# Layer 2 of a two-layer MoE by seven block products: result additions one tile later, first products inside layer 1's last gate, weight steps in another order

## The chip, the cores and the metric

The kernel runs on one core of a Trainium2 chip. The core has a matrix engine (TensorE, "PE" in the rows; its weight loads are "PEld"), VectorE (DVE), ScalarE (ACT), GpSimd (POOL) and SyncE (SP), which here issues nearly all DMAs. Each engine takes its instructions in the order in which the program lists them; they meet only at semaphores. Matmuls write to PSUM, the other data lies in SBUF. The metric is the time of one execution on the device in microseconds (us).

## The reference

```python
attn_out = _attn_ref(q, k, v)                    # 4 x 8 heads, 576 pooled queries, 1152 keys, D = 64
x = attn_out.transpose(0, 2, 1, 3).reshape(2304, 512)
# layer 1
h = x @ w_in                                     # 2304 x 512 by 512 x 2048
x = (h - np.tanh(h)) @ w_out                     # 2048 x 512
# layer 2
h = x @ w2_in
y = (h * (1.0 / (1.0 + np.exp(-1.702 * h)))) @ w2_out
```

Everything is float32, and the kernel keeps nearly that precision: it splits each operand into a rounded high part and the rest (the low part) and multiplies high by high, high by low and low by high.

## The kernel before

The program has three parts: attention, layer 1 and layer 2. The order on each engine is the order in which the Python code emits instructions; jobs are put into lists by hand (`at(step, place, job)` in layer 2, `early(w, place, job)` for jobs that stand inside layer 1's last ten gates) and emitted when that place is reached.

**Layer 1** walks 40 steps w (4 quarters of the 2048 hidden columns, 5 blocks of tokens, 2 halves). In each, TensorE makes `h` (24 matmuls, L1069) and then the output product `y` of two steps earlier (24 matmuls, L1152); `gate` follows on ScalarE and VectorE, `split_g` (L1081 on ScalarE, L1083 on GpSimd) splits the result. L1172 adds `y` into the accumulator `xb`. The `y` of the last two steps is made by `tail`, after layer 2's first `h` products.

**Layer 2** (`second_layer`) has 12 steps i: 4 quarters q of 512 hidden columns times 3 groups of 768 tokens. A group's tokens are two sides of 384 (G); tokens, model columns and hidden columns are each cut in two, and `h` of these blocks is made by seven products instead of eight. The operands are sums and differences of blocks: of x (X1, X2, X3, X4, beside the raw X11, X21, X22) and of the weights (S1 to S4, beside A11, A12, A22).

- `h_product(i, n)`, n = 0 to 6 (L934), is 12 matmuls of 384 columns for each product, into the PSUM tiles a, b, c, b, a, c, b. `h_after(n)` follows each: a copy on ScalarE (L943) and additions on VectorE (L945 to L956) that build up the blocks of `h` in `work`. `h_product` 3 needs tile `b` emptied by L945, 5 needs `c` emptied by L947, 6 needs L949 and L950.
- `gate2` is a sigmoid on ScalarE (L961) and a multiplication on VectorE (L962), four of each a step. `round_g` (L966, ScalarE) and `low_g` (L971, GpSimd) split the result.
- `y_product(i - 1, m)`, m = 0 to 5 (L985), is 12 matmuls of 512 columns for 128 tokens. Two products share a PSUM tile: 0 and 1, 2 and 3, 4 and 5. The addition to the accumulator follows each: L999 on ScalarE in the first quarter (a copy), L1001 on VectorE after that.
- The PSUM pool `ps` has four buffers of two banks each; a, b, c and the three `y` tiles of a step go through them in turn.
- x operands: `combine` (L701, VectorE) forms the sums, `round_x` (L706, L708, ScalarE) makes the high part, `low_x` (L714, L717, GpSimd or VectorE) the low part. `keep` stores the finished operand of each of the three groups in DRAM, `fetch` loads it again for the later quarters.
- Weights: `load_piece` loads 64-bit raw values into one of two buffers (L121), `convert_steps` turns them into float32 in four steps on VectorE (L138, L144, L151, L158) with one on ScalarE (L137), `split` (L165, L166, L765, L766) splits output weights, and `form` combines and splits the input weights of a quarter (L789 combination, L800 high part on ScalarE, L803 low part on GpSimd).

In every step, `go` emits `h_product` and `h_after` 0 to 6 with the jobs of places h0 to h6, the gate, the jobs of y0, and then the six `y` products, each with its addition, with the jobs of y1 to y5. All that the diff moves lies in these places.

Of the kernel before, what the change touches and what calls it, by code (L numbers as in the profile page):

```python
# [28 lines left out]
def tile_pooled_attention_two_moe(  # L29
# [11 lines left out]
    nc = tc.nc  # L41
# [594 lines left out]
    def second_layer(mem, HL, work):  # L636
# [16 lines left out]
        def wops(at):  # L653
# [5 lines left out]
            mem[:, 0:OPX], mem[:, OPX:2 * OPX], mem[:, 2 * OPX:3 * OPX], mem[:, free:free + OPX])]  # L659
        wgroups = [wops(3 * OPX), wops(HL[2])]  # L660
# [4 lines left out]
        u2, u3 = (work[:, 2 * OPX + n * 2 * G:2 * OPX + (n + 1) * 2 * G].rearrange(  # L665
            "p (f t) -> p f t", f=2) for n in range(2))
        sig = u2, u3
# [4 lines left out]
        parks = f32(part(9 * W + OPX, DM)), f32(mem[:, 3 * OPX + 14 * OPW:HL[3]])  # L672
# [11 lines left out]

        raw_x = {X11: (0, 0), X21: (1, 0), X22: (1, 1)}

        def scratch(n, o):
            t = rbd[:, 0:2 * G] if n == 0 else rest[:, 0:2 * G] if o == X1 else rest[:, 2 * G:4 * G]
            return t.rearrange("p (c t) -> p c t", c=2)

        def combine(n, o):
            dst = scratch(n, o)
            get = {(k, side): pieces(n, k, side) for k in range(2) for side in range(2)}
            for i in range(len(groups[n])):
                cols = get[0, 0][i][0]
                x = {at: got[i][1] for at, got in get.items()}
                d = dst[:, :, cols]
# [3 lines left out]
                nc.vector.tensor_tensor(d, one, two, op=op)  # L701
# [26 lines left out]
        def build(n, fast=()):  # L728
            def first(o):
                if o not in raw_x:  # L730
                    combine(n, o)
                round_x(n, o)

            def low(o):
                low_x(n, o, nc.vector if o in fast else nc.gpsimd)
                keep(n, o)

            return lambda o: lambda: first(o), lambda o: lambda: low(o)

        def prepared(kind, qn, f, home=None):  # L740
# [22 lines left out]
            def split():  # L763
                w, t = weight("o", n), home.unsqueeze(1)
# [5 lines left out]
        def form(qn, fp, boxes):  # L770
            w = wgroups[fp]

            def t(j):
                got = held[2 * fp + j] if qn > NQ else f32(boxes[j]["t"][:])
                return got.rearrange("p (k f) -> p k f", k=2)

            def place(o):
                n = {S1: 0, S3: 1, S2: 0, S4: 0}[o] if qn == NQ else o - S1
                t = slack if qn == NQ else rest
                return t[:, n * 256:(n + 1) * 256]  # L780

            def combine_w(*ops):
                for o in ops:
# [5 lines left out]
                    nc.vector.tensor_tensor(place(o), one, two, op=op)  # L789

            def source(a, b):
# [3 lines left out]
                if b > a:  # L795
                    at_ = rest[:, (a - S1) * 256:(b - S1 + 1) * 256]
# [16 lines left out]
            one = [run(combine_w, S1, S3), run(high, S1, S1), run(high, S3, S3)]  # L813
            two = [run(low, S1, S1), run(low, S3, S3), run(high, A11, A12), run(high, A22, A22)]
            three = [run(combine_w, S2), run(high, S2, S2), run(low, S2, S2)]
            four = [run(low, A11, A12), run(low, A22, A22)]
            five = [run(combine_w, S4), run(high, S4, S4), run(low, S4, S4)]
            return one, two, three, four, five
# [15 lines left out]
        for qn in range(NQ, 2 * NQ):  # L834
            ins = [prepared("i", qn, f, held[f] if qn > NQ else None) for f in range(4)]
            outs = [joined(piece("o", qn * 4 + f)) for f in range(2)]
            outs += [prepared("o", qn, f, parks[f - 2])[0] for f in (2, 3)]
            fs = [form(qn, fp, [ins[2 * fp + j][1] for j in range(2)]) for fp in range(2)]
            p = (qn - 1 - NQ) * NG
            if qn == NQ:  # L840
                early(0, "end", outs[0][0])
                early(1, "end", outs[1][0])
                early(2, "convert", outs[0][1], outs[0][2], outs[1][1])
                early(3, "split", outs[0][3])
                early(3, "convert", outs[1][2])
                early(4, "split", outs[1][3])
# [426 lines left out]
```

## Time and profile before

| | |
|---|---|
| median of 3 runs | 1355.37 us (1354.94 to 1356.22) |
| the profiled execution | 1354.87 us; its span, from the first instruction to the last, 1353.1 us |
| TensorE matmul / weight load | 1213.0 us (90%) / 999.5 us (74%) |
| VectorE / ScalarE / GpSimd | 996.0 us (74%) / 650.2 us (48%) / 620.4 us (46%) |
| mean granted TensorE clock | 0.952 |
| attention and layer 1 up to its last four gates | to 749.7 us |
| layer 2's first `h` product / step 3's / step 11's | starts at 801.8 / 960.7 / 1289.9 us |

The shares are means over three parts with different limits: TensorE is near full up to about 750 us and has gaps after that. A matmul counts as busy while it waits for its data to pass through the array, so a busy TensorE need not be at its full pace, and where the granted clock is 0.5 the same work takes twice as long.

### The profile page before, as it was taken

To read this page: it belongs to the slowest core of one execution; us is meant where nothing else is said; L and a number is where in the kernel's file an instruction comes from. 1 tells how busy PE (TensorE), PEld (TensorE's weight loads), DVE (VectorE), ACT (ScalarE), POOL (GpSimd) and SP (SyncE) were. 2 spreads that over 40 slices of the span, in tenths; PEclk is the share of its full clock that TensorE was granted. 3 is DMA by queue.
4 is the path that set the end of the run, shared out by engine and by line. 5 is a ranking of instruction groups with operands and counts; after the bars stand their busy time and mean duration, and the time that the engine had idled before them with its cause. 6 is when DMAs were issued, how large, how long until landed. Compare 5 with 4: busy or idle time off the path is not lost. (4 is left out here: it accounts for less than half of the span.)

```text
span 1353.1 us, 23589 instructions
## 1 busy us (share of the span) xinstructions
PE 1213.0 (90%) x9504; PEld 999.5 (74%) x9504; DVE 996.0 (74%) x1127; ACT 650.2 (48%) x962; POOL 620.4 (46%) x409
## 2 busy tenths in 40 slices
PE   9999999999999999999999956765898588868887
PEld 7777777777778888898898746655787477757775
DVE  6788888888879999999999877956545656643432
ACT  4556655566557776656665553443332222221210
POOL 6788887887861343333323243534233312341211
PEclk9999999999999999999999988777998789988989
DMA  4232232322201011111111024554544356423502
GB/s 141 80 129 80 92 124 79 116 89 93 76 27 56 31 48 47 47 44 35 47 47 47 32 83 181 195 203 193 196 179 158 143 219 225 162 85 136 190 36 78
DMA packets 45837, 144.44 MB, mean 107 GB/s; under 512 B 12960, under 2 KB 13728, under 8 KB 45728
## 3 DMA queue, kind: packets, MB, share of 16 engines
q1 hardware_dynamic: 45184, 142.54, 29.0%
q8 instruction: 75, 1.23, 0.4%
q10 hardware_dynamic: 544, 0.39, 0.1%
q14 instruction: 34, 0.28, 0.1%
HBM read 116.13 MB, written 21.31 MB: 102 GB/s over the span
## 5 line engine op out<-in xcount | busy, mean ns | idle before, releaser
L985 PE MATMUL y<-big,mem 128*128 128x512 f32 x540 | 178.7, 436 | 70.3 <-DVE xb L1001 37.5
L338 DVE TENSOR_REDUCE mt<-mx 128x2 fp32r<-128x1024 f32 (+2 forms) x176 | 195.8, 1136 | 58.9 <-PE mx L326 36.3
L985 PEld LDWEIGHTS y<-big,mem 128*128 128x128 f32 x540 | 112.6, 213 | 105.4 <-DVE xb L1001 40.8
L413 POOL TENSOR_TENSOR sum<-sum,pf 128x576 f32<-128x576 f32 x126 | 185.1, 1469 | 9.9
L1152 PE MATMUL y<-mem,big 128*128 128x512 f32 (+1 forms) x780 | 186.2, 370 | 3.0 <-POOL mem L1083 2.8
L402 ACT ACTIVATE pf<-sc 128x576 f32<-128x576 f32 x288 | 173.9, 653 | 22.3 <-PE sc L396 10.7
L971 POOL TENSOR_TENSOR mem<-work,mem 128x768 fp32r<-128x768 f32 x35 | 67.2, 1936 | 255.6 <-ACT mem L966 255.6
L1152 PEld LDWEIGHTS y<-mem,big 128*128 128x128 f32 x780 | 143.1, 189 | 24.1 <-POOL mem L1083 4.5
L428 PE MATMUL acc<-pf,v 128*32 128x288 f32 x2304 | 146.3, 407 | 0.0
L1001 DVE TENSOR_TENSOR xb<-xb,y 128x512 f32<-128x512 f32 x54 | 37.0, 685 | 115.5 <-PE y L985 115.5
L428 PEld LDWEIGHTS acc<-pf,v 128*32 128x32 f32 x2304 | 71.6, 110 | 65.7 <-ACT pf L402 4.5
L1083 POOL TENSOR_TENSOR mem<-work,mem 128x1024 fp32r<-128x1024 f32 (+1 forms) x39 | 87.0, 2230 | 66.8 <-ACT mem L1081 66.8
L166 POOL TENSOR_TENSOR big<-wt,big 128x512 fp32r<-128x512 f32 x30 | 40.5, 1350 | 151.3 <-ACT big L165 151.3
L1069 PE MATMUL h<-mem,big 128*128 128x512 f32 (+1 forms) x470 | 105.9, 377 | 0.0
L1069 PEld LDWEIGHTS h<-mem,big 128*128 128x128 f32 x470 | 86.9, 188 | 14.2
L396 PE MATMUL sc<-qh,kh 64*128 64x288 f32 x576 | 91.5, 314 | 0.0
L396 PE MATMUL sc<-row,sel 64*128 64x288 f32 x576 | 85.0, 291 | 0.3 <-ACT row L373 0.3
L396 PE MATMUL sc<-qh,kl 64*128 64x288 f32 x576 | 85.0, 291 | 0.0
L396 PE MATMUL sc<-ql,kh 64*128 64x288 f32 x576 | 84.8, 291 | 0.0
L1130 ACT ACTIVATE work<-work 128x1024 f32<-128x1024 f32 (+1 forms) x40 | 39.1, 978 | 94.4 <-DVE work L1128 94.4
L961 ACT ACTIVATE work<-work 128x768 f32<-128x768 f32 x48 | 39.2, 840 | 91.4 <-DVE work L956 86.9
L445 ACT ACTIVATE u<-acc 128x576 f32<-128x576 f32 x30 | 19.6, 653 | 125.6 <-PE acc L437 125.6
(172 smaller groups left out, 2753.9 us busy)
## 6 DMA issues: line engine op xcount, KB each, us to landing
mem<-x SPq DMA_DIRECT2D x36, 768.0 KB
big<-x SPq DMA_DIRECT2D x27, 768.0 KB
raw<-in_moe_w_in_dram SPq DMA_DIRECT2D x32, 512.0 KB
raw<-in_moe_w_out_dram SPq DMA_DIRECT2D x32, 512.0 KB
v<-in_v_dram SPq DMA_DIRECT2D x16, 576.0 KB
x<-mem SPq DMA_DIRECT2D x12, 768.0 KB
kr<-in_k_dram SPq DMA_DIRECT2D x15, 576.0 KB
qr<-in_q_dram SPq DMA_DIRECT2D x15, 576.0 KB
```

The lines of the kernel that those rows point to most:

```text
L166: nc.gpsimd.tensor_tensor(lo, t, f32(hi), op=ALU.subtract)
L338: nc.vector.tensor_reduce(out, src, AX.X, ALU.max, negate=True)
L396: nc.tensor.matmul(sc[:, s, 0:HB], w[r], m[r, xs], start=(n == 0), stop=(n == 3))
L402: nc.scalar.activation(pf, sc[:, :, 0:HB], AF.Exp, scale=SCALE)
L413: nc.gpsimd.tensor_add(out, parts[p, x], new)
L428: nc.tensor.matmul(acc[32 * n:32 * n + 32, 0], pairs[p]["v"][:, s, t, 32 * h:32 * h + 32], new[t][:, s, :], start=(t == 0), stop=(t == KT ...
L961: nc.scalar.activation(sig[fp], h, AF.Sigmoid, scale=1.702)
L971: eng.tensor_tensor(g[:, :, 1], halves[n][:, fp], f32(g[:, :, 0]), op=ALU.subtract)
L985: nc.tensor.matmul(y, gts[2 * side + fp][:, j, r, 128 * t:128 * t + 128], wo[:, p, :], start=(k == 0), stop=(k == len(terms) - 1))
L1069: nc.tensor.matmul(hb[:, j, 0:TBS[b]], wi[:, c, w, :], x[r][c], start=(k == 0), stop=(k == 3 * NKC - 1))
L1083: eng.tensor_tensor(gt[:, :, 1, :], g, f32(gt[:, :, 0, :]), op=ALU.subtract)
L1152: nc.tensor.matmul(ys[m][:, 0:w], wo[j][:, p, m * 128:(m + 1) * 128], g[:, j, r, :], start=(fp == 0 and not low and j == p == 0), stop=(fp ...
```

## The change

The diff has these parts.

1. **y's additions.** In `go`, `y_product` returns its addition, and the addition of product m is emitted after product m + 1, that of the last after all six.
2. **First products in the last gate.** `h_product` 0, 1 and 2 of step 0, with their `h_after`, are emitted inside gate 59 (place "convert" of w = 9) and at its end, and no longer in `go`. TensorE's order stays as it was. In step 0, `h_after` uses parts of `xb[0]` in place of u2 and u3.
3. **x operands.** `build` has three kinds of jobs now (`first` combines, `high`, `low`); the combinations of the second group's X3 and X1 go to GpSimd; the low parts of the second and third group are all GpSimd's (VectorE made X11, X3, X2 and X4); four `keep` DMAs come later (`kept_later`).
4. **Weights.** The first quarter's input weights are loaded and converted two to four gates earlier, their combinations go to GpSimd, and each half `fp` has a scratch of its own (`sums`). Output weight 1 of that quarter is converted in step 0 and no longer in layer 1. The conversions of the next quarters move by some places.
5. **Step 0 and 1.** The split of step 0's gate comes in step 1 (half of it on VectorE), and the jobs of h0 to h6 of step 0 are emitted after products 3 to 6.

```diff
@@ second_layer
-        u2, u3 = (work[:, 2 * OPX + n * 2 * G:2 * OPX + (n + 1) * 2 * G].rearrange(
+        us = tuple(work[:, 2 * OPX + n * 2 * G:2 * OPX + (n + 1) * 2 * G].rearrange(
             "p (f t) -> p f t", f=2) for n in range(2))
...
-        slack = work[:, 12 * TB:]
+        sums = work[:, 3 * OPX:]
...
+        kept_later = {(2, X1): (1, "y4"), (2, X21): (1, "y5"), (2, X4): (2, "h1"), (2, X22): (2, "h1")}
...
         def build(n, fast=()):
             def first(o):
-                if o not in raw_x:
-                    combine(n, o)
+                combine(n, o, nc.gpsimd if n == 1 and o in (X1, X3) else nc.vector)
+
+            def high(o):
                 round_x(n, o)
...
             def place(o):
-                n = {S1: 0, S3: 1, S2: 0, S4: 0}[o] if qn == NQ else o - S1
-                t = slack if qn == NQ else rest
-                return t[:, n * 256:(n + 1) * 256]
+                n = {S1: 6, S3: 7, S2: 6, S4: 6}[o] if qn == NQ else 4 * fp + o - S1
+                return sums[:, n * 256:(n + 1) * 256]
+
+            eng = nc.gpsimd if qn == NQ else nc.vector
...
-                    nc.vector.tensor_tensor(place(o), one, two, op=op)
+                    eng.tensor_tensor(place(o), one, two, op=op)
...
-                for f in range(4):
-                    early(2 + f, "end", ins[f][0][0])
-                early(4, "convert", ins[0][0][1], ins[0][0][2], ins[1][0][1])
-                early(5, "convert", ins[1][0][2])
-                early(6, "start", *fs[0][0])
...
-                early(9, "start", *fs[1][0], *fs[1][1])
-                early(9, "split", *fs[1][2])
-                early(9, "convert", *fs[1][3], *fs[1][4])
-                plan = ((outs[2], 0, "h1", "h2"), (outs[3], 0, "h5", "y1"))
+                for w, f in ((0, 0), (1, 1), (2, 2), (3, 3)):
+                    early(w, "end", ins[f][0][0])
+                early(2, "convert", ins[0][0][1], ins[0][0][2], ins[1][0][1])
+                early(3, "convert", ins[1][0][2])
+                for w, js in ((4, fs[0]), (8, fs[1])):
+                    early(w - 1, "end", *js[0])
+                    early(w, "start", *js[1])
+                    early(w, "convert", *js[2])
+                    early(w + 1, "convert", *js[3])
...
+                plan = ((outs[1], 0, "h2", "h3"),)
...
+        early(9, "convert", *first(X4), lambda: h_product(0, 0), lambda: h_after(0, 0),
+              *high(X4), *low(X4), lambda: h_product(0, 1), lambda: h_after(0, 1),
+              lambda: h_product(0, 2))
+        early(9, "end", lambda: h_after(0, 2), *high(X22), *low(X22))
         for n in range(1, NG):
-            first, low = build(n, (X11, X3, X2, X4))
...
+            first, high, low = build(n, ())
...
+        first_u = xb[0][:, 0:2, :], xb[0][:, 2:4, :]
+
+        def h_after(i, n):
+            u2, u3 = us if i > 0 else first_u
...
         def go(tail):
+            adds = []
             for i in range(NP + 1):
                 if i < NP:
                     for n in range(7):
-                        h_product(i, n)
-                        h_after(n)
+                        if i > 0 or n > 2:
+                            h_product(i, n)
+                            h_after(i, n)
+                        if n == 2 and i == 1:
+                            low_g(0, nc.vector)
                         if n == 0 and i > 0:
                             round_g(1)
                             low_g(1)
-                        do(i, f"h{n}")
+                            if i == 1:
+                                round_g(0)
+                        if i > 0:
+                            do(i, f"h{n}")
+                        elif n > 2:
+                            for m in ((0,), (1, 2), (3, 4), (5, 6))[n - 3]:
+                                do(i, f"h{m}")
...
                 for m in range(6):
                     if i > 0:
-                        y_product(i - 1, m)()
-                    if m == 2 and i < NP:
+                        adds.append(y_product(i - 1, m))
+                        if m > 0:
+                            adds.pop(0)()
+                    if m == 2 and 0 < i < NP:
                         round_g(0)
                         low_g(0)
                     if m > 0:
                         do(i, f"y{m}")
+                if adds:
+                    adds.pop(0)()
```

The lines of the changed kernel are numbered anew: `y_product`'s matmul is L1011 there, its addition L1027, `h_product` L957, `h_after` L971 to L982, `combine` L704, the low parts of x L717 and L720, of weights L814, layer 1's additions L1212.

First, TensorE's queue at the first `y` tile of step 4 (y_10848 before, y_10847 after), with the semaphores that its instructions wait for. Before, from inside product 0 to the second tile:

```order
L985 MATMUL y_10848<-big,mem 128x512 [waits Pool_49] x2
L985 MATMUL y_10848<-big,mem 128x512 x4
L985 MATMUL y_10848<-big,mem 128x512 [waits DVE_49]
L985 MATMUL y_10848<-big,mem 128x512 x11
L985 MATMUL y_10880<-big,mem 128x512 [waits PE_49]
L985 MATMUL y_10880<-big,mem 128x512 x11
L985 MATMUL y_10880<-big,mem 128x512 [waits DVE_49]
```

After, from the same place on:

```order
L1011 MATMUL y_10847<-big,mem 128x512 [waits Activation_49] x2
L1011 MATMUL y_10847<-big,mem 128x512 x2
L1011 MATMUL y_10847<-big,mem 128x512 [waits Pool_49] x2
L1011 MATMUL y_10847<-big,mem 128x512 x16
L1011 MATMUL y_10878<-big,mem 128x512 [waits DVE_49]
L1011 MATMUL y_10878<-big,mem 128x512 x13
```

The wait for VectorE at the thirteenth matmul of a tile, the start of the odd product, is gone; one stands at the first matmul of the next tile, whose buffer others read before.

Second, VectorE's queue in gate 59, layer 1's last, and at layer 2's first products (`xb_69` is layer 1's result of token block 3, `rbd` a scratch, `b` and `c` PSUM tiles of `h`). Before:

```order
L701 TENSOR_TENSOR rbd<-rbd,xb_66 128x768
L789 TENSOR_TENSOR work<-wt 128x256 x2
L1111 SCALAR_TENSOR_TENSOR work<-work,h 128x2x384
L789 TENSOR_TENSOR work<-work,wt 128x256
...
L1172 TENSOR_TENSOR xb_69<-xb_69,y 128x512 x3
L789 TENSOR_TENSOR work<-wt,work 128x256
...
L701 TENSOR_TENSOR rbd<-xb_66,rbd 128x768
L1083 TENSOR_TENSOR mem<-work,mem 128x2x384
L945 TENSOR_TENSOR work<-rbd,b 128x768
```

After:

```order
L1151 SCALAR_TENSOR_TENSOR work<-work,h 128x2x384
...
L1212 TENSOR_TENSOR xb_69<-xb_69,y 128x512 x3
L704 TENSOR_TENSOR xb_67<-xb_66,rbd 128x2x384
L971 TENSOR_TENSOR xb_66<-rbd,b 128x768
L1168 SCALAR_TENSOR_TENSOR work<-work 128x2x384
L1171 SCALAR_TENSOR_TENSOR work<-work 128x2x384
L1173 COPY_PREDICATED work<-work 128x2x384
L973 TENSOR_TENSOR xb_66<-xb_66,c 128x768
L1123 TENSOR_TENSOR mem<-work,mem 128x2x384
```

The weight combinations (L789) have left VectorE, and the first addition of `h` stands before the gate's last three instructions and before the split, not after them.

Third, GpSimd's queue at the turn from gate 59 to step 0. Before:

```order
L717 TENSOR_TENSOR mem<-rbd,mem 128x768
L714 TENSOR_TENSOR mem<-xb_67,mem 128x768
L717 TENSOR_TENSOR mem<-work,mem 128x768
L714 TENSOR_TENSOR mem<-xb_67,mem 128x2x128
L714 TENSOR_TENSOR mem<-xb_68,mem 128x2x256
L714 TENSOR_TENSOR mem<-xb_69,mem 128x2x128
L714 TENSOR_TENSOR mem<-xb_68,mem 128x2x256
```

After:

```order
L720 TENSOR_TENSOR mem<-xb_67,mem 128x768
L717 TENSOR_TENSOR mem<-xb_67,mem 128x768
L704 TENSOR_TENSOR work<-xb_69 128x2x128
L704 TENSOR_TENSOR work<-xb_68 128x2x256
L704 TENSOR_TENSOR work<-xb_69,xb_67 128x2x128
L704 TENSOR_TENSOR work<-xb_68 128x2x256
L717 TENSOR_TENSOR big<-xb_67,big 128x2x128
L717 TENSOR_TENSOR big<-xb_68,big 128x2x256
L720 TENSOR_TENSOR big<-work,big 128x768
L720 TENSOR_TENSOR mem<-work,mem 128x768
L166 TENSOR_TENSOR big<-wt,big 128x512
L720 TENSOR_TENSOR big<-work,big 128x768
```

Between the end of the first group's operands and the first split of layer 2's gate, GpSimd now also has two combinations of the second group, its low parts that were VectorE's, and an output weight's split.

## Rows read from the trace of the kernel before

**Rows 1.** Busy time by stretch: engines' busy us (instructions), granted clock, DMA share, GB/s.

```profile
core 0 of [0], span 1353.1 us
...
700.00:750.00 50.00, 50.00 (x245) 44.23 (x244) 46.66 (x55) 30.94 (x39) 15.42 (x9) 1.00 0.16 53
749.72:801.79 52.07, 44.22 (x194) 36.60 (x192) 41.12 (x44) 26.93 (x34) 20.80 (x13) 0.93 0.14 56
801.79:960.67 158.88, 102.14 (x446) 90.17 (x444) 108.09 (x125) 61.74 (x92) 64.40 (x39) 0.81 0.44 169
960.67:1349.40 388.73, 320.81 (x1477) 276.28 (x1475) 194.78 (x234) 92.31 (x128) 100.71 (x58) 0.92 0.42 156
```

**Rows 2.** Timeline of TensorE in layer 1: start, us, instruction, count.

```profile
700.27 4.32 PE L1069 MATMUL h<-big 128*128 128x384 f32 x24
704.43 4.32 PE L1152 MATMUL y<-mem,big 128*128 128x384 f32 x24
...
749.72 5.60 PE L1069 MATMUL h<-mem,w 128*128 128x512 f32 x24
755.16 0.62 PE L1152 MATMUL y<-mem,w 128*128 128x512 f32 x2
```

**Rows 3.** TensorE's waits, 960.67 to 1353.1 us: total us, times, longest.

```profile
PE y L985 <- DVE xb L1001: 62.4, 25, 13.3
PE y L985 <- ACT xb L999: 3.8, 3, 2.4
PE y L985 <- ACT wa L137: 1.7, 2, 0.9
```

**Rows 4.** TensorE's waits, 749.72 to 960.67 us.

```profile
PE y L985 <- ACT xb L999: 28.2, 6, 14.6
PE a L934 <- POOL mem L803: 8.2, 1, 8.2
PE b L934 <- DVE work L945: 7.1, 2, 4.6
...
PE y L1152 <- POOL mem L1083: 2.0, 2, 1.2
```

**Rows 5.** Chain that ended last, in step 9: start, us, what.

```profile
1226.62 0.96 DVE work L956
...
1229.48 0.85 ACT work L961
...
1230.35 1.83 DVE work L962 x2
```

**Rows 6.** Timeline of TensorE, step 9, two odd `y` products: idle before and releaser.

```profile
1232.83 0.80 PE L985 MATMUL y<-w,mem 128*128 128x512 f32 x1 [3.49 <-DVE xb L1001]
...
1242.03 0.47 PE L985 MATMUL y<-w,mem 128*128 128x512 f32 x1 [0.87 <-DVE xb L1001]
```

**Rows 7.** Busy time by stretch, around these two products; columns as above.

```profile
1232.80:1238.20 5.40, 5.37 (x13) 4.22 (x14) 0.00 (x0) 0.00 (x0) 0.00 (x0) 0.50 0.00 0
1242.00:1247.00 5.00, 4.97 (x22) 4.15 (x23) 0.69 (x1) 0.00 (x0) 2.47 (x2) 1.00 0.02 5
```

**Rows 8.** Timeline of GpSimd and VectorE in step 1.

```profile
859.00 6.53 POOL L971 TENSOR_TENSOR mem<-work,mem 128x768 fp32r<-128x768 f32 x3
...
863.90 2.17 DVE L144 SCALAR_TENSOR_TENSOR wt<-raw,wt 128x512 int32<-128x512 int32 x1
...
900.32 0.69 DVE L144 SCALAR_TENSOR_TENSOR wt<-raw,wt 128x512 int32<-128x512 int32 x1
```

**Rows 9.** VectorE by line, 801.79 to 960.67 us: busy us, mean ns, idle before.

```profile
L158 DVE SCALAR_TENSOR_TENSOR wt<-raw,wt 128x512 int32<-128x512 int32 x10 | 12.5, 1246 | 0.3
...
L144 DVE SCALAR_TENSOR_TENSOR wt<-raw,wt 128x512 int32<-128x512 int32 x10 | 9.9, 994 | 0.3
```

**Rows 10.** Timeline of VectorE, where step 5's weights are combined.

```profile
1063.41 0.93 DVE L789 TENSOR_TENSOR work<-w 128x256 f32<-128x256 f32 x1 [3.60 <-POOL mem L803]
```

**Rows 11.** GpSimd by line and shape, 960.67 to 1349.40 us; columns as in rows 9.

```profile
L803 POOL TENSOR_TENSOR mem<-work,mem 128x1024 fp32r<-128x1024 f32 x4 | 9.4, 2356 | 9.6 <-ACT mem L800 9.6
L803 POOL TENSOR_TENSOR mem<-w,mem 128x512 fp32r<-128x512 f32 x4 | 5.9, 1478 | 20.0 <-ACT mem L800 20.0
```

**Rows 12.** Timeline of VectorE, the last addition.

```profile
1349.45 0.69 DVE L1001 TENSOR_TENSOR xb<-xb,y 128x512 f32<-128x512 f32 x1 [3.11 <-PE y L985]
```

More of the change, by code (lines that the diff above doesn't have):

```diff
@@ L658, in second_layer @@
             part(3 * W, OPX), part(3 * W + OPX, OPX), part(9 * W, OPX),
-            mem[:, 0:OPX], mem[:, OPX:2 * OPX], mem[:, 2 * OPX:3 * OPX], mem[:, free:free + OPX])]
-        wgroups = [wops(3 * OPX), wops(HL[2])]
+            *(mem[:, 7 * OPW + n * OPX:7 * OPW + (n + 1) * OPX] for n in range(3)),
+            mem[:, free:free + OPX])]
+        wgroups = [wops(0), wops(HL[2])]
         gts = [t.rearrange("p (j r t) -> p j r t", j=2, r=2) for t in (
@@ L700, in combine @@
                     X2: (d, x[0, 0], ALU.add), X4: (x[1, 0], d, ALU.subtract)}[o]
-                nc.vector.tensor_tensor(d, one, two, op=op)
+                eng.tensor_tensor(dst[:, :, cols], one, two, op=op)
         def round_x(n, o):
@@ L735, in low, with each @@
                 low_x(n, o, nc.vector if o in fast else nc.gpsimd)
-                keep(n, o)
-            return lambda o: lambda: first(o), lambda o: lambda: low(o)
+                if (n, o) not in kept_later:
+                    keep(n, o)
+            def each(fn):
+                return lambda *some: [lambda o=o: fn(o) for o in some]
+            return each(first), each(high), each(low)
         def prepared(kind, qn, f, home=None):
@@ L812, in form @@
                         + [run(low, *x) for x in parts])
[L813 to L818, printed above, removed]
+            return (
+                [run(combine_w, S1, S3)],
+                [run(high, S1, S1), run(high, S3, S3), run(high, A11, A12), run(high, A22, A22),
+                 run(low, S1, S1), run(low, S3, S3), run(combine_w, S2)],
+                [run(high, S2, S2), run(low, A11, A12), run(low, S2, S2), run(combine_w, S4),
+                 run(low, A22, A22)],
+                [run(high, S4, S4), run(low, S4, S4)])
         jobs = {}
@@ L839, in second_layer @@
+            fs = [form(qn, fp, [ins[2 * fp + j][1] for j in range(2)], homes)
+                  for fp in range(2)]
             p = (qn - 1 - NQ) * NG
             if qn == NQ:
[L841 to L846, printed above, removed]
-                for f in range(4):
-                    early(2 + f, "end", ins[f][0][0])
@@ new lines, in second_layer @@
+        early(5, "end", *first(X1))
+        early(6, "convert", *high(X1, X11), *low(X1))
+        early(6, "end", *low(X11), *first(X3))
+        early(7, "convert", *high(X3, X21), *low(X3))
+        early(7, "end", *low(X21), *first(X2))
+        early(8, "convert", *high(X2), *low(X2))
+        early(9, "convert", *first(X4), lambda: h_product(0, 0), lambda: h_after(0, 0),
+              *high(X4), *low(X4), lambda: h_product(0, 1), lambda: h_after(0, 1),
+              lambda: h_product(0, 2))
@@ L917, in second_layer @@
+        for (n, o), place in kept_later.items():
+            at(*place, lambda n=n, o=o: keep(n, o))
         for i in range(NG, NP):
```

100 lines of the change are left out of this document (52 added, 48 removed).

## The prediction

> **What bounds the kernel now.** I first cut the span into stages with the table of busy time by stretch [rows 1]. From 700 to 750 us, in the middle of layer 1, TensorE is busy all the time at a granted clock of 1.00. From 749.72 us on it is not: 44.2 of 52.1 us, then 102.1 of 158.9 (the turn from layer 1 to layer 2: steps 0 to 2), then 320.8 of 388.7 (steps 3 to 11). No other engine is near full in the last two stretches: VectorE 108.1 and 194.8, GpSimd 64.4 and 100.7. So after 749.72 us the kernel is bound neither by TensorE nor by another engine, but by TensorE's waits.
>
> What TensorE's own work would need is read from gap-free stretches. 24 matmuls of 512 columns take 755.16 - 749.72 = 5.44 us, and 24 of 384 columns 704.43 - 700.27 = 4.16 us [rows 2]. Layer 2 runs both shapes. Seven products `h` of 12 matmuls are 7 x 2.08 = 14.56 us; six products `y` of 12 are 6 x 2.72 = 16.32 us; a step is 30.88 us. Against that pace:
> - 749.72 to 801.79 holds the last four gates' `h` (two pieces of 512 columns, two of 384) and four `y` of 512, 24 matmuls each: 6 x 5.44 + 2 x 4.16 = 40.96 us. It took 52.07: 11.1 too many.
> - 801.79 to 960.67 holds step 0's seven products, layer 1's last two `y` (8.32) and two whole steps: 84.64 us. It took 158.88: 74.2 too many.
> - 960.67 to 1349.40 holds eight whole steps, the last seven `h` products and twelve `y`: 8 x 30.88 + 14.56 + 32.64 = 294.2 us. It took 388.73: 94.5 too many.
>
> Together 179.8 us that are no work of TensorE's. The lists of waits say for whom [rows 3, 4]. From 960.67 on it is almost only L1001, the addition of a `y` tile: 25 waits, 62.4 us. Before that it is ScalarE's addition L999 (28.2 us in 6 waits), then weight operands (L803), h's additions (L945) and layer 1's own work.
>
> The timeline of one ordinary step shows how a short addition costs that much [rows 6]. The second `y` product of a pair (1232.83) sat 3.49 us until L1001, and later odd products 0.87 us. The chain of that moment [rows 5] reads backwards: `y` waited for L1001, which stood on VectorE behind the gate (L962), which waited for ScalarE's sigmoid L961, which waited for L956, the last addition of `h`. TensorE needed none of these; it waited because products 0 and 1 share a PSUM tile and the addition of 0 was queued before product 1. Then comes the second price: after the 3.49 us wait the granted clock is 0.50 for 5.4 us (1.2 instead of 2.4 GHz), 2.7 us lost; around a wait of 0.87 us it stays 1.00 [rows 7].
>
> **What the change does, and its cost.**
> *The additions one tile later.* In the order before, every odd product waits for VectorE; in the order after only the first product of a tile does, for the tile's former readers. An addition now waits until both halves are written and is wanted when its PSUM buffer comes round again: six tiles a step go through four buffers, so `b` of the next step needs the buffer of products 0 and 1. Between the end of product 1 and that `b` lie four products and `a`, 4 x 2.72 + 2.08 = 13 us. The gate and its wait, 3.5 us, hide in that. No instruction is added. For steps 3 to 11 I take away all 94.5 us, and add again one short wait of 0.87 us in each of seven steps (3 to 9, where weights are still split and formed): 6 us. The two ends are 0, and a full 3.49 + 2.7 in each of eight steps, 50 us; the nearest row is the short one, since no `h` product waits in the list from 960.67 on.
> The price moves to the end: the last pair's two additions now both follow the last matmul, one more of 0.69 us [rows 12].
>
> *The form step.* Where weights are combined, before, VectorE waited 3.60 us for GpSimd, as both halves used one scratch [rows 10]; now each has its own. GpSimd's six subtractions, 2 x 2.36 + 2 x 1.48 and two smaller ones, under 10.7 us [rows 11], start during `y` products that last 16.3 us, so they fit.
>
> *Transfers.* The same bytes move in less time: steps 3 to 11 had 156 GB/s at a share of 0.42; in 294 us it is 206 GB/s, 0.56. Steps 0 to 2 had 0.44 and would have 0.44 x 158.9 / 102 = 0.69 [rows 1]. Not full, so I cost it at nothing; a late transfer would show as TensorE waiting for DMA, and [rows 3] has none.
>
> *The turn.* PE's order is the same. What moves is who prepares what, and when: weight block 0 of fp 0 and 1 is formed on GpSimd one or more gates earlier, the first x operands too; the first three `h` products' additions stand inside the last gate, so L945's late place (7.1 us of waits) and the weight wait (8.2) have no cause left [rows 4]. One weight block's conversion leaves layer 1 for step 0. The price: GpSimd takes over eight subtractions and two combinations of x from VectorE.
> That is where I expect a rest. In the trace the conversion step L144 takes 0.69 us alone and 2.17 while three GpSimd instructions of 6.53 us run [rows 8]; over the turn L144 has a mean of 0.994 and L158, of the same size, 1.246, that is 0.30 and 0.56 more, with GpSimd busy 64.4 / 158.9 = 0.41 of the time [rows 1, 9]. Per instruction with two SBUF inputs that is 0.7 to 1.4 us at a GpSimd that is always busy; I take 0.9, near the lower end, as the gate's multiplications stayed at 0.92 (two in 1.83) where GpSimd rested [rows 5].
> The Trainium skill ("SBUF — State Buffer", SBUF: two separate sides) says that VectorE instructions with two SBUF inputs and GpSimd's take turns on one port pair, whole instructions at a time; these rows agree. It speaks against moving work to GpSimd, and by it alone each such instruction would wait for one of GpSimd's.
> Between product 6 of step 0 and the additions that free the buffer for step 1's `c`, VectorE has about ten instructions of that kind (four conversion, four gate, two combination) at 0.7 to 0.95 us, L956 (0.96) and four additions of at most 0.69: 8 + 1 + 2.8 = 11.8 us. TensorE covers 8.32 + 2 x 2.08 = 12.5. GpSimd has some eleven instructions of 768 columns from the last gate on, at 6.53 / 3 = 2.18 each 24 us of about 28, a share of 0.85. With 10 x 0.9 x 0.85 = 7.6 us more they are 6.9 late, and the clock drop adds 2.7: 9.6. Step 1 has a similar list with fewer deadlines; I take 7.4. Together 17 us; the ends are 0, and the doubled price of all conversions (below).
> In layer 1's end I keep the waits for GpSimd (2.0 [rows 4]) and 1 us: 3.
>
> *Sum*, against the profiled execution, 1354.87 us (its span 1353.1 and 1.8 around it; the median is 1355.37, 0.5 more): 1354.87 - 11.1 - 74.2 - 94.5 + 0.7 = 1175.8, plus 3 + 17 + 6 = 1202.
>
> **The rivals.**
> *A. Nothing is left over.* TensorE runs gap-free to the end: 1176 to 1183. For it: each wait listed loses its cause. Against it: VectorE's 11.8 us under a cover of 12.5.
> *B. The turn becomes bound by VectorE and GpSimd together.* Steps 0 to 2 hold 9 conversions of four instructions; if each takes the 2.17 us of [rows 8] instead of the 1.12 that L144 and L158 have in the mean, VectorE needs 36 x 1.05 = 38 us more than its 108.1, less about 10 for the ten instructions that GpSimd takes over (at L956's 0.96): 136 instead of 84.6 us. Time: 1176 + 51 + 9 = 1236. This is the skill's rule taken to its end; the trace bears it out for single instructions, not for whole stages, as GpSimd also idles on ScalarE.
> *C. The wait comes back in every step*, at a PSUM buffer or an operand: an addition that stands behind the gate and a late conversion, and `b` or `c` of the next step waits. At the old price, 8 x (3.49 + 2.7) = 50 on top: 1252. For it: VectorE still works in order. Against it: 13 us of cover.
> *D. Slower: the clock.* If a TensorE that never rests were granted 1.2 GHz, its 379 us of work in the last two stretches (84.6 + 294.2) would take up to 379 more. It decides at 40%: (1355 - 1202) / 379. Against it: 50 us of full work at 1.00 in layer 1 [rows 1].
>
> **How the numbers follow.** The forecast, 1202, has 0.62, with its own range 1183 to 1222; A 0.07, B 0.20, C 0.08, D 0.03. All but D are far faster than the 0.2% (2.7 us) that a measurement of this kernel can tell from no change; D I split into 0.02 slower and 0.01 same. The range that holds 8 in 10 reaches from 1180 (part of A) to 1245 (most of B).
>
> **What would show it.** Right: from step 3 on, starts of `a` 31 us apart, no wait for L1001's successor over 1 us, clock 1.00 through the steps; TensorE's busy share after 750 us over 0.9; the last addition pair after the last matmul. The rest should stand at `c` or `b` of step 1 and in front of `y` of step 0, with VectorE's conversion steps near 2 us beside a busy GpSimd. Wrong: waits for DMA in the `h` products (fetches too late), waits of 3 us or more at a tile's first product in steps 3 to 11 (C), or a turn over 125 us (B).

## The result, and the profile after

The changed kernel takes 1218.29 us (median of 4 runs, 1217.81 to 1218.86) against 1355.48 (4 runs, 1354.94 to 1356.22): a ratio of 0.8988, 95% interval 0.8972 to 0.9003. Forecast: 1202, range 1180 to 1245. The profiled execution took 1217.97, its span 1216.2.

Lines are those of the changed kernel from here on: y's product is L1011 and its additions L1025 (ScalarE) and L1027 (VectorE), h's products are L957 and their additions L971 to L982, the gate's multiplication L988, the low parts of the gated values L997 and of the x operands L717 and L720, weights are combined at L800 and their low parts made at L814, a conversion is L138, L144, L151 and L158, and layer 1's last additions are L1212 (L1157 is an operation of its gate on VectorE).

Busy time by stretch of the changed kernel, columns as in [rows 1]: layer 1's end, the turn in three pieces (each ends where the next `a` starts) and as a whole, and steps 3 to 11:

```profile
749.72:798.34 48.62, 44.10 (x198) 36.97 (x196) 47.24 (x43) 28.69 (x38) 33.23 (x21) 0.96 0.25 92
798.34:827.88 29.54, 26.05 (x134) 25.47 (x132) 26.51 (x25) 13.43 (x21) 24.46 (x16) 0.88 0.39 140
827.88:870.69 42.81, 33.86 (x157) 29.38 (x157) 42.41 (x39) 19.92 (x27) 27.33 (x15) 0.92 0.48 174
870.69:914.40 43.71, 33.39 (x157) 29.59 (x156) 39.09 (x41) 20.77 (x34) 22.18 (x12) 0.92 0.74 289
798.34:914.40 116.06, 93.30 (x445) 84.44 (x444) 108.00 (x103) 54.11 (x81) 73.96 (x43) 0.91 0.56 209
914.40:1211.80 297.40, 295.86 (x1477) 266.15 (x1475) 205.67 (x243) 95.78 (x136) 113.93 (x63) 1.00 0.55 207
```

Steps 3 to 11 went from 388.73 us at a clock of 0.92 to 297.40 at 1.00, 3.2 above TensorE's own 294.2; from step 4 on `a` starts every 30.94 or 30.95 us. The turn went from 158.88 to 116.06, 31.4 above its 84.64. In the turn's second piece VectorE, the third pair of numbers, is busy for 42.41 of 42.81 us: a full engine stands behind TensorE's waits.

TensorE's waits in steps 3 to 11 of the changed kernel, in total, times and longest, where 25 waits of 62.4 us for L1001 stood [rows 3]:

```profile
PE b L957 <- DVE work L971: 1.1, 1, 1.1
PE b L957 <- DVE work L976: 0.2, 1, 0.2
PE c L957 <- ACT xb L1025: 0.2, 1, 0.2
```

The turn's long waits, from TensorE's timeline of the changed kernel (idle time before and releaser in brackets):

```profile
803.74 4.18 PE L957 MATMUL b<-big,mem 128*128 128x384 f32 x12 [3.13 <-DVE work L1157]
...
840.19 3.92 PE L957 MATMUL c<-big,mem 128*128 128x384 f32 x12 [6.67 <-DVE xb L1212]
...
876.04 2.38 PE L957 MATMUL b<-big,mem 128*128 128x384 f32 x12 [3.08 <-ACT xb L1025]
...
888.05 3.89 PE L957 MATMUL b<-mem 128*128 128x384 f32 x12 [6.62 <-DVE work L971]
```

Twelve matmuls of 384 columns start 2.08 us before the next product at full clock, and their row then shows 2.24 to 2.27; after three of these waits the row shows 3.9 to 4.2. The wait at 876.04 is put down to ScalarE, but leads back to VectorE as well: ScalarE's copy L1025 stands in its queue behind a rounding that had waited for VectorE's combination L704.

```profile
872.89 0.84 ACT L711 ACTIVATE mem<-work 128x768 fp32r<-128x768 f32 x1 [1.95 <-DVE work L704]
...
875.40 0.59 ACT L1025 ACTIVATE xb<-y 128x512 f32<-128x512 f32 x1
```

Of the 31.4 us, 22.8 are idle time (116.06 - 93.30) and 8.7 are TensorE's busy time above 84.64, most of it at a lower clock.

What the last long wait stands for is seen on VectorE and GpSimd just before it, in the timeline of the changed kernel:

```profile
877.90 6.47 POOL L997 TENSOR_TENSOR mem<-work,mem 128x768 fp32r<-128x768 f32 x3
878.42 2.05 DVE L138 TENSOR_SCALAR wt<-raw 128x512 int32<-128x512 int32 x1
880.50 2.20 DVE L144 SCALAR_TENSOR_TENSOR wt<-raw,wt 128x512 int32<-128x512 int32 x1
882.81 2.10 DVE L151 SCALAR_TENSOR_TENSOR wt<-wa,wt 128x512 f32<-128x512 f32 x1
884.33 2.25 POOL L997 TENSOR_TENSOR big<-work,big 128x768 fp32r<-128x768 f32 x1
...
884.95 2.18 DVE L158 SCALAR_TENSOR_TENSOR wt<-raw,wt 128x512 int32<-128x512 int32 x1
887.05 0.94 DVE L971 TENSOR_TENSOR work<-rbd,b 128x768 f32<-128x768 f32 x1
887.92 0.41 DVE L138 TENSOR_SCALAR wt<-raw 128x512 int32<-128x512 int32 x1
...
888.37 0.69 DVE L144 SCALAR_TENSOR_TENSOR wt<-raw,wt 128x512 int32<-128x512 int32 x1
```

One half of a weight conversion took 8.5 us (2.05 + 2.20 + 2.10 + 2.18) beside four operations of GpSimd; the first two operations of the next one, with GpSimd at rest, took 0.41 and 0.69. L971, for which TensorE waited, came right behind. At the end, the last two additions follow the last matmul, as predicted (1.28 us for both, against 0.69 in [rows 12]):

```profile
1211.81 1.28 DVE L1027 TENSOR_TENSOR xb<-xb,y 128x512 f32<-128x512 f32 x2 [4.16 <-PE y L1011]
```

### The profile page after: what moved, and what is told of

It is laid out like the page before. It is cut to its first block, busy times and chain, and to the rows that moved or that the text cites. A ratio compares the mean times of both kernels' runs of the same rounds, so it can differ in the third digit from the quotient of the medians.

```text
span 1216.2 us, 23601 instructions
## 1 busy us (share of the span) xinstructions
PE 1177.7 (97%) x9504; PEld 982.8 (81%) x9504; DVE 1010.9 (83%) x1108; ACT 648.4 (53%) x962; POOL 663.5 (55%) x428
## 4 chain that ended last, share of the span: by engine, by line
PE 74%; DVE 17%; ACT 4%; issue 2%; POOL 1%; DMA 1%; DVEq 0%; SPq 0%; POOLq 0%; ACTq 0%
PE y L1011 13%; PE sc L396 13%; PE acc L428 11%; PE h L1109 10%; PE y L1192 9%; PE b L957 5%; PE a L957 3%; PE mx L326 3%; PE c L957 3%; PE acc L437 3%; DVE wt L144 2%; DVE wt L151 2%; DVE work L1168 2%; DVE wt L158 1%; DVE work L1151 1%
## 5 line engine op out<-in xcount | busy, mean ns | idle before, releaser
L1011 PE MATMUL y<-big,mem 128*128 128x512 f32 x540 | 153.7, 390 | 1.2 <-ACT big L774 1.0
L997 POOL TENSOR_TENSOR mem<-work,mem 128x768 fp32r<-128x768 f32 x33 | 65.4, 2000 | 131.9 <-ACT mem L992 131.9
L1011 PEld LDWEIGHTS y<-big,mem 128*128 128x128 f32 x540 | 101.1, 188 | 22.6 <-ACT big L774 1.5
L158 DVE SCALAR_TENSOR_TENSOR wt<-raw,wt 128x512 int32<-128x512 int32 x64 | 75.3, 1177 | 2.0
```

What stands on the lines that cost most here:

```text
L158: nc.vector.scalar_tensor_tensor(out=t, in0=raw[:, :, 0], scalar=29, in1=t, op0=ALU.logical_shift_right, op1=ALU.bitwise_or,)
L997: eng.tensor_tensor(g[:, :, 1], halves[n][:, fp], f32(g[:, :, 0]), op=ALU.subtract)
L1011: nc.tensor.matmul(y, gts[2 * side + fp][:, j, r, 128 * t:128 * t + 128], wo[:, p, :], start=(k == 0), stop=(k == len(terms) - 1))
```

## The experiments

Theory: the lag of y's additions gives back the steps; the rest of the gain is the turn's, and the turn stays bound by VectorE, which GpSimd slows. Rivals: the order alone decides where TensorE waits; or VectorE's load alone does. Times are medians of 4 runs (the last run: 5), ratios are to the kernel before in the same session.

**1. The lag alone**, on the kernel before:

```diff
-                        y_product(i - 1, m)()
+                        adds.append(y_product(i - 1, m))
+                        if m > 0:
+                            adds.pop(0)()
```

> The kernel before with one part of the change alone: y's additions one tile later in layer 2. Theory 1 (steps 3 to 11 give about 94 us back by the lag alone, and the waits of the y products inside the turn go too, some 15 us more, while the form's wait of 3.6 us and the rest of the turn stay): 1235 to 1265 us, about 1250, and no wait of a y product over 1 us in steps 4 to 10. Rival (the lag only works together with the new order of operands, so that other waits appear where the additions' waits were): over 1285 us. Rival (the turn and layer 1's end are bound up with the lag as well): under 1235 us.

Measured: 1255.98 us, ratio 0.9271 [0.9255, 0.9286]. The lag alone is 99.2 of the 137 us. Turn, and steps 3 to 11, of this kernel:

```profile
801.93:933.52 131.59, 97.16 (x445) 88.53 (x444) 106.40 (x119) 55.78 (x83) 58.66 (x36) 0.86 0.53 202
933.52:1249.00 315.48, 301.03 (x1477) 271.18 (x1475) 207.10 (x240) 97.02 (x138) 111.69 (x62) 0.98 0.51 192
```

The turn lost 27.3 us, not 15, and the steps 73.3, not the 94 expected. What stays in the steps are mainly three waits, in steps 3, 6 and 9 (L945 and L1001 are L971 and L1027 of the changed kernel):

```profile
947.54 4.21 PE L934 MATMUL b<-mem 128*128 128x384 f32 x12 [7.49 <-DVE work L945]
...
1043.88 3.91 PE L934 MATMUL c<-big,mem 128*128 128x384 f32 x12 [3.39 <-DVE xb L1001]
...
1141.97 3.50 PE L934 MATMUL c<-big,mem 128*128 128x384 f32 x12 [3.38 <-DVE xb L1001]
```

**2. The change without the lag** (the same lines, undone in the changed kernel).

> The changed kernel with y's additions issued right behind each product, as before. Theory 1: the odd products' wait of 3.49 us and the five of 0.87 us come back in every step from 1 on, with the clock at its lower level behind them: about 9 us a step in steps 3 to 11 and some in steps 1 and 2: 1300 to 1325 us. Rival (the new order alone would have removed most of the waits): under 1270 us. If the parts add up, this run's loss against the changed kernel equals the gain of the lag alone against the kernel before.

Measured: 1324.69 us, ratio 0.9778 [0.9764, 0.9793]: 106.4 slower than the changed kernel. TensorE's waits in steps 4 to 11 of it:

```profile
PE y L1011 <- DVE xb L1027: 52.2, 25, 8.1
```

Again 25, as in [rows 3]. The other parts alone give 30.5 us; 99.2 + 30.5 falls 7.5 short of the whole of 137.2, so the parts help each other a little. Where the other parts gain and lose is seen by setting the changed kernel beside run 1: step 0 is 18.1 us shorter (29.54 against 47.62), step 1 2.5, layer 1's end 3.6, steps 3, 6 and 9 together 18, but step 2 is 5.0 us longer (43.71 against 38.71). Step 2 takes 31.35 us in run 7, so most of its excess hangs on GpSimd's low parts.

**3. One place for both forms' weight sums**, as before:

```diff
-  ... else 4 * fp + o - S1
+  ... else o - S1
...
-                    at_ = sums[:, 4 * fp * 256:4 * (fp + 1) * 256]
+                    at_ = sums[:, 0:4 * 256]
```

> The changed kernel with one place for the weight sums of both column pairs of a form in layer 2's later quarters, as before, instead of one for each. The lag alone showed waits of 3.39 us before c, with 1.6 us of lower clock behind each, in two steps with forms. Theory (these waits come from the second form's sums waiting for the first one's reads, with y's additions behind them on VectorE): they come back, 5.3 us each in steps 6 and 9, and perhaps a third in the turn's last step: 1227 to 1236 us. Rival (the order of the conversions decides and the place of the sums does not): 1217 to 1220 us.

Measured: 1232.74 us, ratio 0.9094 [0.9076, 0.9112], 14.5 slower. The wait of run 1 is back, in steps 6 and 9; here is step 6, VectorE first, TensorE below:

```profile
1009.68 0.95 DVE L800 TENSOR_TENSOR work<-w 128x256 f32<-128x256 f32 x1 [3.66 <-POOL mem L814]
...
1020.41 1.87 DVE L1027 TENSOR_TENSOR xb<-xb,y 128x512 f32<-128x512 f32 x3
```

```profile
1021.14 4.21 PE L957 MATMUL c<-big,mem 128*128 128x384 f32 x12 [3.38 <-DVE xb L1027]
```

VectorE waits 3.66 us for GpSimd to read the first form's sums, with y's additions queued behind; the lag moves that lateness to the `c` of the next step. Each of these two steps takes 37.1 us instead of 30.95; step 3 takes 35.8 instead of 33.3.

**4. The wait before step 1's `c` taken away by order alone**: layer 1's last products and additions are issued right behind the last h product of step 0, ahead of a half conversion and the gate.

```diff
+                        if i == 0 and n == 6:
+                            tail()
...
-                if i == 0:
-                    tail()
```

> The changed kernel with the last additions of layer 1 (L1212) put on VectorE ahead of half a weight conversion, the gate and a combination of step 0 instead of behind them, about 9 us of its queue. TensorE's order is unchanged. Theory VectorE-bound (it is busy 42.4 of 42.8 us from 827.88 to 870.69, so a wait that is taken away here comes back behind the next VectorE result): the wait of 6.67 us before c of step 1 goes, but another of 4 to 6 us stands before the next product that needs L971 or L975, and the time falls by only 0 to 4 us: 1214.5 to 1218.5. Rival (order alone): the wait of 6.67 us and the 1.8 us of lower clock behind it go and nothing comes back: 1208.5 to 1211.

Measured: 1218.33 us, ratio 0.8992 [0.8978, 0.9005]: no change. In TensorE's timeline of it the wait has moved on by one product:

```profile
834.19 2.24 PE L957 MATMUL c<-big,mem 128*128 128x384 f32 x12
843.17 4.21 PE L957 MATMUL b<-mem 128*128 128x384 f32 x12 [6.74 <-DVE work L971]
```

6.67 us went and 6.74 came: moving these additions forward gains nothing by itself. The new wait is not all a full VectorE, though. Just before L971 VectorE itself stood idle, for ScalarE's copy L969, which is queued behind a rounding that waits for VectorE's L704:

```profile
842.16 0.95 DVE L971 TENSOR_TENSOR work<-rbd,b 128x768 f32<-128x768 f32 x1 [1.66 <-ACT rbd L969]
```

So part of the turn is a chain through both queues; whether another order of ScalarE's queue would help was not run.

**5. The first products outside the last gate**: L971 of step 0 stands behind the gate's operations.

```diff
-  ... lambda: h_product(0, 0), lambda: h_after(0, 0), ... lambda: h_product(0, 2))
...
-                        if i > 0 or n > 2:
-                            h_product(i, n)
-                            h_after(i, n)
+                        h_product(i, n)
+                        h_after(i, n)
```

> The changed kernel with the first three products of layer 2 and what follows them on ScalarE and VectorE issued behind the last gate of layer 1 instead of inside it. TensorE's order is the same; what moves is L971's place on VectorE, behind three operations of the gate (about 4 us). Theory VectorE-bound: the second b of step 0 waits about 3 us longer, VectorE itself does the same work, and the time rises by 0 to 4 us: 1218 to 1222 us. Rival (the early products carry the gain at layer 1's end): over 1225 us.

Measured: 1218.30 us, ratio 0.8989 [0.8976, 0.9003]. In its timeline of TensorE (L955 and L969 are L957 and L971 here) a wait appears in step 0, and step 2 begins all the same at 871.65, against 870.69:

```profile
816.55 4.00 PE L955 MATMUL b<-mem 128*128 128x384 f32 x12 [7.44 <-DVE xb L969]
...
871.65 2.27 PE L955 MATMUL a<-big,mem 128*128 128x384 f32 x12
```

In return the wait before step 1's `c` fell from 6.67 to 1.88 us. It cost nothing because VectorE had the same work to do. So this place of the additions gains nothing by itself.

**6. Three conversions later in VectorE's queue.**

```diff
-                    (ins[2][0], 1, "y3", "y4"), (ins[3][0], 2, "h1", "h2"),
-                    (outs[0], 2, "h4", "h5"), ...
+                    (ins[2][0], 2, "h1", "h2"), (ins[3][0], 2, "h3", "h4"),
+                    (outs[0], 2, "h5", "h6"), ...
```

> The changed kernel with three weight conversions of VectorE moved back in its queue: one from ahead of L971 of step 2 to behind it, and the two after it by two or three products each. TensorE's order is unchanged. Theory VectorE-bound with some slack here (39.1 of 43.7 us busy from 870.69 to 914.40): the wait of 6.62 us before the second b of step 2 falls under 2 us, but the moved conversions delay the weight forms at step 2's end, whose results step 3 needs, so that 1 to 5 us remain of the 8: 1213 to 1217 us. Rival (order alone): 1208.5 to 1211 us.

Measured: 1227.06 us, ratio 0.9057 [0.9043, 0.9070]: 8.8 slower, which no theory had forecast. The wait of 6.62 us is gone, as expected, but the weights of step 3 come late:

```profile
913.01 1.01 PE L957 MATMUL a<-big,mem 128*128 128x384 f32 x2 [5.30 <-ACT mem L811]
...
922.26 1.65 PE L957 MATMUL a<-big,mem 128*128 128x384 f32 x4 [3.25 <-POOL mem L814]
```

With two smaller waits they come to 10.9 us. The forms are a chain over three engines behind the last conversion. The expectation had named the late forms, but from VectorE's slack had put them at 3 to 7 us, without the two engines behind it.

**7. GpSimd's load taken away.** The low parts of the x operands of groups 1 and 2 are left out (their products read what lay there before).

```diff
-                low_x(n, o, nc.vector if o in fast else nc.gpsimd)
+                if n == 0:
+                    low_x(n, o, nc.vector if o in fast else nc.gpsimd)
```

> The changed kernel without the low parts of the layer-2 operands of token groups 1 and 2: some 14 operations of GpSimd of 1.8 to 2.9 us in steps 0 and 1 are left out (their products then read what lay there before). VectorE's instructions are the same. Theory contention (VectorE's operations between two SBUF tiles are slower beside GpSimd): VectorE's busy time from step 0 to the end of step 2 falls from 108 us to 88 to 98, with the means of the conversion and gate operations near 0.7 and 0.95 us, and the time falls to 1198 to 1212 us. Rival (VectorE's load and its order alone): VectorE's busy time stays at 105 to 109 us and the time at 1216 to 1219 us.

Measured: 1200.26 us, ratio 0.8859 [0.8846, 0.8872], 18.0 faster. The turn, and one conversion operation by line (busy us, mean ns), of this kernel:

```profile
799.90:895.25 95.35, 88.52 (x446) 80.18 (x445) 88.10 (x102) 53.66 (x79) 38.17 (x25) 0.98 0.67 253
```

```profile
L158 DVE SCALAR_TENSOR_TENSOR wt<-raw,wt 128x512 int32<-128x512 int32 x8 | 5.5, 693 | 0.3
```

The same row of the changed kernel's turn:

```profile
L158 DVE SCALAR_TENSOR_TENSOR wt<-raw,wt 128x512 int32<-128x512 int32 x8 | 13.6, 1694 | 0.3
```

VectorE, with the same instructions, is busy 19.9 us less, and the turn is 20.7 us shorter. Not every operation gains: L138's mean rose from 0.93 to 1.19 us beside what GpSimd still does. GpSimd's busy time falls by 35.8 us (73.96 - 38.17), and VectorE's by 19.9: 0.56 us for each, a net figure of this turn. (The expectation counted fourteen operations; in the trace they are seventeen instructions, and an eighteenth, of L814, only falls outside the stretch. One wait of 1.05 us for an operand goes as well.)

**8. The gate's multiplications of steps 0 and 1 on GpSimd.**

```diff
-                    gate2(0)
-                    gate2(1)
+                    gate2(0, nc.gpsimd if i < 2 else nc.vector)
+                    gate2(1, nc.gpsimd if i < 2 else nc.vector)
```

> The changed kernel with the gate's multiplications (L988) of steps 0 and 1 on GpSimd instead of VectorE: eight operations, 9.0 us of VectorE in the changed kernel's trace, 1.8 to 2.3 us each on GpSimd. Theory contention (VectorE and GpSimd slow each other between SBUF tiles, so that work moved from one to the other is paid for by both): 1214 to 1225 us, about the changed kernel's time, with VectorE's conversions slower than before. Rival (VectorE's load alone): about 9 us less load on the bound engine: 1208 to 1212 us.

Measured: 1219.60 us, ratio 0.8999 [0.8985, 0.9012]: no gain. The turn of this kernel:

```profile
798.07:915.92 117.85, 93.56 (x446) 84.40 (x444) 109.88 (x96) 54.80 (x81) 92.67 (x51) 0.93 0.54 206
```

VectorE has eight operations (9.0 us) fewer (seven in the row, as one more falls inside the stretch) and is busier, 109.88 against 108.00. At 0.56 us for each of GpSimd's 18.7 more, 108.0 - 9.0 + 10.5 = 109.5 was to be expected.

**9. The gate as one ScalarE function, and work back from GpSimd.** Three kernels: the gate alone, the low parts of run 7 on VectorE alone, and both.

```diff
-                nc.scalar.activation(us[fp], h, AF.Sigmoid, scale=1.702)
-                nc.vector.tensor_mul(h, h, us[fp])
+                nc.scalar.activation(h, h, AF.Gelu_apprx_sigmoid)
```

```diff
-                low_x(n, o, nc.vector if o in fast else nc.gpsimd)
+                low_x(n, o, nc.vector if n > 0 else nc.gpsimd)
```

> The changed kernel with the gate of layer 2 as a single ScalarE function (x times sigmoid of 1.702 x) instead of a sigmoid on ScalarE and a multiplication on VectorE: 48 VectorE operations leave, 12 of them (12.7 us) between step 0 and the end of step 2. Theory VectorE-bound in the turn: the turn of 116.1 us loses 8 to 14 us: 1204 to 1211 us; steps 4 to 11, where VectorE is about 70% busy and TensorE waits for nothing, gain nothing. Rival (the turn waits for chains of latency and not for VectorE's load): 1214 to 1219 us.

> The changed kernel with the low parts of the layer-2 operands of token groups 1 and 2 on VectorE instead of GpSimd. Without them the turn lost 20.7 us (95.35 against 116.06); on VectorE fourteen operations of 0.95 us come to 13.3 us more of its queue. Theory contention (one GpSimd operation beside VectorE costs VectorE more than doing it itself): VectorE's busy time in the turn is 98 to 104 us against 108.0, and the time falls to 1208 to 1215 us. Rival (VectorE's own load decides): 13 us more load on the bound engine: 1228 to 1232 us.

> The run before together with the gate of layer 2 as a single ScalarE function. If the two gains add up (7.6 us for the gate, 4 to 8 us for the low parts): 1201 to 1207 us. If VectorE is no longer the bound of the turn after one of them, the second gives little: 1207 to 1211 us.

Measured: 1210.69 us (0.8934 [0.8920, 0.8949]), 1214.44 (0.8963 [0.8950, 0.8977]) and 1206.37 (0.8901 [0.8886, 0.8916]): 7.6, 3.9 and 11.9 faster than the changed kernel. The gains add up. The turn of the second kernel:

```profile
798.66:911.93 113.27, 93.76 (x446) 85.64 (x445) 103.75 (x121) 54.82 (x81) 41.41 (x26) 0.89 0.57 217
```

VectorE carries the seventeen instructions more (the eighteenth in the row is at the stretch's edge) and is busy 4.25 us less. The gate's gain is at the low end of what I expected: VectorE is busy 11.3 us less in the turn of that kernel (96.70 against 108.00), and the turn is 6.8 us shorter (109.25). So the turn does not follow VectorE's work one for one.

**10. The low parts of the gated values, too**, between steps 1 and 2, on top of both:

```diff
-                            low_g(1)
+                            low_g(1, nc.vector if i == 2 else nc.gpsimd)
...
-                        low_g(0)
+                        low_g(0, nc.vector if i == 1 else nc.gpsimd)
```

> The run with the low parts on VectorE and the gate as one ScalarE function, and beside it the four low parts of the gated values between steps 1 and 2 on VectorE instead of GpSimd. In that run's trace they took 9.0 us of GpSimd at step 2's start, beside which four conversion operations of VectorE took 8.6 us instead of the 2.5 us of the same four a little later, and L971 behind them came 3.44 us late. Theory contention: VectorE has four operations of 0.95 us more and 6.1 us of lengthening less, L971 comes about 2.3 us earlier, and the wait of 3.44 us falls to about 1: 1201 to 1205 us. Rival (more operations in VectorE's queue ahead of L971, which now wait for ScalarE's high parts too): 1206 to 1210 us.

Measured: 1203.35 us (1202.21 to 1203.68), ratio 0.8878 [0.8866, 0.8890], the fastest kernel here that leaves nothing out. VectorE and TensorE in its timeline, at the place of the 8.5 us above (L996 is L997 there):

```profile
867.80 1.83 DVE L996 TENSOR_TENSOR mem<-work,mem 128x768 fp32r<-128x768 f32 x2
...
870.87 0.42 DVE L138 TENSOR_SCALAR wt<-raw 128x512 int32<-128x512 int32 x1
871.33 0.69 DVE L144 SCALAR_TENSOR_TENSOR wt<-raw,wt 128x512 int32<-128x512 int32 x1
872.12 0.69 DVE L151 SCALAR_TENSOR_TENSOR wt<-wa,wt 128x512 f32<-128x512 f32 x1
872.85 0.69 DVE L158 SCALAR_TENSOR_TENSOR wt<-raw,wt 128x512 int32<-128x512 int32 x1
...
876.67 2.37 PE L957 MATMUL b<-mem 128*128 128x384 f32 x12 [1.65 <-DVE work L971]
```

The four operations take 2.7 us from first to last, and the wait fell from the 3.44 us of the kernel with both to 1.65. The turn (799.65 to 901.49) is still 17.2 us above TensorE's 84.64; what that rest waits for was not taken apart.

## Why the prediction was right, and where it was off

By its own sum, 1354.87 - 11.1 - 74.2 - 94.5 + 0.7 and the three residuals:

- **Steps 3 to 11: right in size, wrong in cause.** 6 us were to remain; 3.2 did, 2.4 of them in step 3. But I gave all 94.5 us to the lag. Run 1 shows 73.3 for it. The form's own scratch, which I had described and given no price, is worth 10.5 to 12.3 us in steps 6 and 9 (they take 36.2 us each in run 1 and 37.1 in run 3). The third wait of run 1, 7.49 us in step 3, is 1.14 in the changed kernel; I take the other order of the weight steps for the cause, but no run undid it alone.
- **The last pair**: 0.7 predicted; from the last matmul's stretch to the span's end 4.4 us against 3.7.
- **The turn: mechanism right, place right in part, size too small.** I put 6.9 us of waiting and 2.7 of clock before step 1's `c`; 6.67 and about 1.7 stood there. That this came so near is in part luck: between the end of step 0's product 6 and L1212 VectorE had fifteen conversion, gate and combination instructions, not ten, and with two of h's additions they took 19.5 us (819.64 to 839.13). At the times that the same shapes take elsewhere in this trace (0.41 to 0.95 us) that would be some 12 us, an estimate, so some 7 us of lengthening fell on fifteen instructions, where I had put 7.6 on ten. In front of step 0's `y`, the other place named, nothing waited. For the rest of the turn I guessed a round 7.4, which makes 17 in all, and it is 31.4: 6.7 in step 0, where I had none (the wait stood before its first `b`), 11.9 in step 1, 12.8 in step 2. VectorE was not late at one place; from 827.88 to 870.69 it was full, as rival B said, and run 4 shows that a wait taken away there returns behind VectorE's next result. B's price, every conversion operation at 2.17 us, was too high: L144 has a mean of 1.52 and L158 of 1.69 in the turn, and VectorE's sum stayed at 108.0. With 22 instructions fewer than in the kernel before (103 against 125) that is the same busy time as its 108.09 [rows 1]: the shorter queue freed nothing.
- **GpSimd's part**: run 7 shows it, run 8 as well from the other side. The 17 us should have been worked out over all of the turn: the 43 instructions and 74 us of GpSimd there, come to 41 of VectorE's 108 us if 0.56 holds for all of them.
- **Layer 1's end**: 3 predicted, 7.7 measured. Of these 0.9 arose earlier (the gate that began at 749.72 before begins at 750.62), 4.5 are waits in `y` (2.62, 1.48 and 0.42), the rest mostly lower clock. VectorE is busy 47.24 of 48.62 us there, 6.1 more than before with one instruction fewer, and GpSimd 33.23, 12.4 more [rows 1]: about 0.5 us for each, so it looks like the turn; I ran nothing that tells, and in runs with the same code the stretch ended between 798 and 801 us.
- **First products inside the gate**: I said that L945's late place and the weight wait had no cause left. In step 0 both went (in step 2 L971 now makes TensorE wait 6.62 us), but the early place of the additions is not what gains: run 5 puts L971 back behind the gate, 7.44 us of wait return, and the time is the same. I take the earlier weight forms for what gains in step 0; no run undid them alone.
- **Rivals**: A (1176 to 1183) fell to the turn; C fell as a wait in every step, as no `b` or `c` waits after step 3, but its mechanism was there: 3.08 us before `b` of step 2, for a `y` addition that came too late (L1025), and 3.4 us in steps 6 and 9 of runs 1 and 3; D fell, the clock was 1.00 in steps that have no rest.

The Trainium skill ("SBUF — State Buffer", SBUF: two separate sides) says that GpSimd's instructions and VectorE's with two SBUF inputs, or in a two-port mode, take the shared port pair for a whole instruction each. The traces agree as far as they go: L138, with one input, took 2.05 us there instead of 0.41, while L973, which reads PSUM, took 0.94 us (844.51) inside a GpSimd operation of 2.31 us (843.99). What the mode of L138 is no trace shows.

## What to carry to other kernels

Before moving work from a full VectorE to GpSimd, price what it does to VectorE: here each microsecond of GpSimd cost VectorE 0.56, net, and seventeen instructions moved back made the kernel 3.9 us faster. When a wait is taken away by order, look for the engine that was full before it; here one was, the wait came back at the next product, and what helped was less work on that engine. An addition can be issued as late as its buffer allows, but whatever stands ahead of it in its queue (here a form that waits for GpSimd) is then seen by a different consumer, one step later.

## What was not expected of the hardware

The price of contention was larger than the work itself: seventeen low parts cost VectorE 19.9 us while on GpSimd and 15.7 us (103.75 - 88.10) when it did them itself. And the clock's answer to a rest was not always the same: after 3.08 us of waiting twelve matmuls took 2.38 us (876.04), after 3.13 us 4.18 (803.74).
